# Re-timing a kernel of attention and two-layer products: first-block products among the first layer groups, scores behind quarters of w_out, batch 2's projection ten groups later with k and v loaded first

## The chip, the cores and the metric

One core of a Trainium2 chip. The metric is the device time of one execution in microseconds (us), median over runs. Executions are called fast when they are not in a slower state of the chip. "The trace" is one profiled execution; its span is some 1.8 us shorter than the time.

## The reference

```python
k_proj = einsum('ks,bhsd->bhkd', E, k)          # 1024 keys become 64
v_proj = einsum('ks,bhsd->bhkd', F, v)
attn   = softmax(q @ k_proj^T / 8) @ v_proj     # 8 batches, 8 heads, head size 64
x = attn, heads side by side                    # 8192 tokens x 512
h = x @ w_in                                    # 512 -> 2048
out = (h * clip(h + 3, 0, 6) / 6) @ w_out       # 2048 -> 512
```

All inputs are float32. The kernel computes in bfloat16 with float32 accumulation.

## The kernel before

Tokens go in blocks of 512, two to a batch. A **layer group** is four matmuls of one block against 128 columns of w_in, an activation on ScalarE (r) and a multiplication on VectorE (g); 16 groups make a block's first product. The second product (w_out) takes four rows of 16 matmuls, called here in **quarters** of four matmuls each. While batch b is multiplied, batch b+1's attention is spread between its groups by a generator: each `next(ahead)` is one **call**, one after each group and one after each row of w_out.

```python
ps_mm = ...tile_pool(name="ps_mm", bufs=4, PSUM)   # accumulators of the layer
ps_at = ...tile_pool(name="ps_at", bufs=4, PSUM)   # accumulators of the attention: pat()

class Attention:
    def project(self, ps): ...       # 8 matmul pairs: k and v to 64 rows, into one pat() tile
    def keys_out(self, ps): ...      # 2 VectorE copies of k out of that tile
    def values_out(self, ps): ...    # 2 VectorE copies of v out of that tile
    def scores(self, j, alloc): ...  # 8 matmuls into two pat() tiles, 2 exponentials on ScalarE
    def normalised(self, j):         # sums and values of one pair of heads: four pat() tiles
        den = self.quads(ones...); av = self.quads(vp...)
        lns = [log(den[t]) for t in range(NB)]
        yield
        for t in range(NB):
            nc.vector.tensor_mul(self.xT[:, j, t, :], av[t], inverse(lns[t]))
            yield
    def steps(self, plan):
        ps = pat(); self.project(ps)
        yield
        self.keys_out(ps); self.values_out(ps)
        yield
        self.keys_transposed_dma()                 # kT, a transposing DMA on SyncE's queue
        if self.b == 1: qT_dma[1] = q_transposed(1)
        if self.b + 1 < B:
            nc.gpsimd.tensor_copy(mark, ...)       # waits for qT (batch 1) or kT, then
            load_kqv(self.b + 1)                   # the next batch's q, k, v
        ...                                        # then the plan: (calls to wait, part, pair)

# first block of batch 0: fillers (matmuls on ones, thrown away) keep TensorE going
def busy(n): ...
    ...
    products(0); self.vals(1, nc.vector.tensor_copy); busy(2)
    products(1); self.vals(2, nc.scalar.copy); busy(2)
    products(2); self.vals(3, nc.scalar.copy); busy(2)
    products(3)
```

The softmax here doesn't subtract the row's maximum and nothing guards it: scores larger than these inputs give would overflow.

## Time and profile before

| | before |
|---|---|
| time, median of 4 | 525.78 us (525.38 to 526.23) |
| span of the trace | 523.8 us |
| TensorE busy | 510.6 us |
| idle TensorE apart from the first 1.5 us and the end (4.3), of which for v | some 7.4 us, 3.2 |
| mean granted clock | 0.997 |

A page line such as "PE 510.6 (97%) x2811" is busy time, share of the span and instructions. PE is TensorE, PEld its weight loads, DVE VectorE, ACT ScalarE, POOL GpSimd; L210 is line 210 of that run's kernel, so the same line has different numbers in different runs. A wait line gives engine, tile and line, what it waited for, the sum, the count and the longest. A timeline line gives start, duration, engine, source line, operation, output and inputs, shape and count, and in brackets the idle time before it with what ended it. The lines of the kernel before stand in the prediction.

### The profile page before, as it was taken

The page shows a single profiled execution, that of the slowest core. Times are in us where ns is not written, and L with a number is a line of the kernel's source. Part 1 is how long each engine was busy: PE and PEld are TensorE (multiplying, and loading weights), DVE is VectorE, ACT ScalarE, POOL GpSimd, SP SyncE. Part 2 cuts the span into 40 slices and gives each one's busy share as a digit, 9 for nine tenths or more (in the row PEclk, how much of TensorE's full clock was granted, in tenths as well). Part 3 has the DMA queues.
Part 4 walks back from the last instruction along what each step waited for, and adds up shares of the span by engine and source line. Part 5 has one row for each costly group of instructions (what it writes and reads, how often), then busy time and mean ns, then how long its engine had stood idle before and what let it go on. Part 6 is the DMA issues. An engine that isn't in the chain of part 4 may idle for free.

```text
span 523.8 us, 7239 instructions
## 1 busy us (share of the span) xinstructions
PE 510.6 (97%) x2811; PEld 223.9 (43%) x2811; DVE 237.9 (45%) x376; ACT 281.8 (54%) x518; POOL 37.3 (7%) x56
## 2 busy tenths in 40 slices
PE   8999989699999999999999999999999999999996
PEld 4444433344444444444444444444444444444442
DVE  3482734464553552553454454535435544444420
ACT  3565465296546763566436664467635765444431
POOL 8510020020020000200002000200000000000000
PEclk9999999899999999999999999999999999999999
DMA  9999699699229811595018941299111110111112
GB/s 173 202 205 207 137 161 216 127 150 161 73 58 199 176 43 40 93 218 122 32 38 144 186 97 40 56 190 182 46 41 31 41 41 21 41 41 42 40 41 80
DMA packets 73683, 55.40 MB, mean 106 GB/s; under 512 B 35504, under 2 KB 65456, under 8 KB 73648
## 3 DMA queue, kind: packets, MB, share of 16 engines
q0 software_dynamic: 31424, 29.36, 35.6%
q1 hardware_dynamic: 42000, 25.17, 18.6%
q8 instruction: 22, 0.36, 0.3%
q10 hardware_dynamic: 224, 0.39, 0.3%
q14 instruction: 13, 0.11, 0.1%
HBM read 59.24 MB, written 16.78 MB: 145 GB/s over the span
## 4 chain that ended last, share of the span: by engine, by line
PE 89%; DMA 5%; DVE 2%; ACT 1%; issue 1%; POOL 0%; SPq 0%; DVEq 0%; ACTq 0%
PE mm L402 40%; PE mm L422 39%; DMA v<-in_v_dram 4%; PE at L180 3%; PE at L216 2%; PE mm L84 1%; PE at L202 1%; DMA qT<-q 1%; DVE g L408 1%; PE at L320 0%; DVE kp L186 0%; ACT r L407 0%; ACT ln L158 0%; PE at L272 0%; PE at L288 0%
## 5 line engine op out<-in xcount | busy, mean ns | idle before, releaser
L408 DVE SCALAR_TENSOR_TENSOR g<-r,mm 128x512 bf16<-128x512 f32 x256 | 172.4, 685 | 215.7 <-ACT r L407 215.3
L402 PE MATMUL mm<-xT,w_in_sb 128*128 128x512 bf16 x1024 | 236.4, 380 | 1.3 <-DVE g L408 1.3
L422 PE MATMUL mm<-w_out_sb,g 128*128 128x512 bf16 x1024 | 231.3, 379 | 0.0
L407 ACT ACTIVATE r<-mm 128x512 f32<-128x512 f32 x256 | 152.0, 604 | 70.8 <-PE mm L402 68.2
L402 PEld LDWEIGHTS <-w_in_sb 128*128 128x128 bf16 x1024 | 97.1, 98 | 126.7 <-issue 15.6
L422 PEld LDWEIGHTS <-g 128*128 128x128 bf16 x1024 | 98.9, 98 | 121.1 <-issue 3.8
L436 ACT COPY o_sb<-mm 128x512 f32<-128x512 f32 x59 | 34.5, 585 | 143.4 <-PE mm L422 143.4
L227 DVE TENSOR_TENSOR xT<-at,rec 128x512 bf16<-128x512 f32 x56 | 38.0, 684 | 24.3 <-ACT rec L163 24.3
L163 ACT ACTIVATE rec<-ln 128x512 f32<-128x512 f32 x60 | 37.6, 638 | 0.0
L158 ACT ACTIVATE ln<-at 128x512 f32<-128x512 f32 x60 | 33.0, 615 | 7.6 <-PE at L216 4.5
L207 ACT ACTIVATE aT<-at 128x512 bf16<-128x512 f32 x56 | 28.9, 611 | 2.3 <-PE at L202 2.3
L244 POOL COPY mark<-kT 1x1 bf16<-1x1 bf16 x5 | 0.9, 176 | 250.0 <-DMA kT<-kp 250.0
L180 PE MATMUL at<-v,f_t 128*64 128x512 bf16 x56 | 14.6, 407 | 3.2 <-DMA v<-in_v_dram 3.2
L180 PE MATMUL at<-k,e_t 128*64 128x512 bf16 x56 | 14.6, 404 | 0.0
L216 PE MATMUL at<-aT,vp 64*64 64x512 bf16 x112 | 12.3, 378 | 0.4 <-DVE xT L227 0.2
L84 PE MATMUL mm<-ones 128*128 128x512 bf16 x27 | 10.1, 482 | 1.5 <-DVE ones L77 1.5
L216 PE MATMUL at<-aT,ones 64*64 64x512 bf16 x112 | 11.5, 400 | 0.0
L180 PEld LDWEIGHTS <-e_t 128*64 128x64 bf16 x56 | 5.8, 113 | 10.2 <-issue 6.5
L202 PE MATMUL at<-qT,kT 64*64 64x256 bf16 x224 | 8.8, 275 | 1.3 <-DMA qT<-q 1.3
L190 DVE CAST vp<-at 64x512 bf16<-64x512 f32 x14 | 9.7, 694 | 0.3
L186 DVE CAST kp<-at 64x512 bf16<-64x512 f32 x14 | 8.9, 674 | 0.0
L216 PEld LDWEIGHTS <-ones 64*64 64x64 bf16 x112 | 3.2, 103 | 11.9 <-issue 11.9
(57 smaller groups left out, 110.2 us busy)
## 6 DMA issues: line engine op xcount, KB each, us to landing
out_dram<-o_sb SPq DMA_DIRECT2D x63, 256.0 KB, 2.0
k<-in_k_dram POOLq DMA_DIRECT2D x7, 1024.0 KB, 15.0
v<-in_v_dram POOLq DMA_DIRECT2D x7, 1024.0 KB, 20.5
q<-in_q_dram POOLq DMA_DIRECT2D x7, 1024.0 KB, 9.9
w_out_sb<-in_moe_w_out_dram POOLq DMA_DIRECT2D x4, 512.0 KB, 17.7
w_in_sb<-in_moe_w_in_dram POOLq DMA_DIRECT2D x3, 512.0 KB, 12.1
k<-in_k_dram POOLq DMA_DIRECT2D x4, 256.0 KB, 5.4
v<-in_v_dram POOLq DMA_DIRECT2D x4, 256.0 KB, 7.5
```

The source lines that it names most:

```text
L84: nc.tensor.matmul(ps, ones[:, :P], ones, start=True, stop=True)
L158: nc.scalar.activation(ln, den, AF.Ln)
L163: nc.scalar.activation(rec, ln, AF.Exp, scale=-1.0)
L180: nc.tensor.matmul(ps[e * KP:(e + 1) * KP], ef_t[e][:, so, :], kqv[self.b]["kv"[e]][:, :, so, :], start=(so == 0), stop=(so == SO - 1))
L207: nc.scalar.activation(self.aT[j][:, r].rearrange("p a n -> p (a n)"), tiles[r], AF.Exp, scale=scale)
L216: nc.tensor.matmul(tiles[t][c:c + D].rearrange("p (r n) -> p r n", r=2), stationary(r, 2 * j + a), self.aT[j][r:r + KP, :, a, :], start=Tr ...
L227: nc.vector.tensor_mul(self.xT[:, j, t, :], av[t], inverse(lns[t]))
L402: nc.tensor.matmul(h_ps, w_in_sb[:, ko, fo * P:(fo + 1) * P], xT[:, ko, t, :], start=(ko == 0), stop=(ko == KO - 1))
L407: nc.scalar.activation(r, h_ps, AF.Relu, bias=0.5, scale=1.0 / 6.0)
L408: nc.vector.scalar_tensor_tensor(g[:, fo, :], r, 1.0, h_ps, op0=ALU.min, op1=ALU.mult)
L422: nc.tensor.matmul(o_ps, g[:, fo, c * P:(c + 1) * P], w_out_sb[:, fo, :], start=(fo == 0), stop=(fo == FO - 1))
L436: (copy or nc.scalar.copy)(o_sb, o_ps)
```

## The change

Four things are intended: real work instead of fillers in the first block, scores asked for later so that VectorE and the transposing DMA have finished, batch 2's v landed before it is projected, and VectorE's copies out of the projection spread out. The plan becomes a table of parts with the number of calls to wait before each.

```diff
+            if self.b + 1 < B:
+                mark = ...
+                load_kqv(self.b + 1, "qkv" if self.b > 1 else "kvq")
...
+    PLANS = {1: ((0, "project"), (0, "keys_out"), (1, "turn"), (0, "values_out", 0), (2, "values_out", 1),
+                 (1, "two_scores", 0), (3, "two_scores", 2), (1, "normalised", 0),
+                 (0, "normalised", 1), (0, "normalised", 2), (0, "normalised", 3)),
+             2: ((10, "project"), (0, "keys_out"), (1, "turn"), (2, "values_out", 0), (3, "values_out", 1),
+                 (1, "two_scores", 0), (2, "two_scores", 2), (3, "normalised", 0),
+                 (0, "normalised", 1), (1, "normalised", 2), (0, "normalised", 3))}
...
             scores(KO - 1)
+            self.vals(0, nc.vector.tensor_copy)
             sums(KO - 2)
-            busy(1)
-            self.vals(0, nc.vector.tensor_copy)
+            self.vals(1, nc.vector.tensor_copy)
+            products(0)
             sums(KO - 1)
...
+            products(2)
             self.vals(3, nc.scalar.copy)
-            busy(2)
+            yield                       # the last product comes between the first groups' matmuls
             products(3)
...
-    first.second_scores()
+    ahead = Attention(1, x_next).steps(PLANS[1])
     rows = [second_group(0, 0, g[0], c) for c in range(SB)]
     for i in range(SB + 1):
         for c in range(SB - 1):
             next(rows[c], None)
-        if i < 2:
-            first.second_values(2 * i)
+        if i == 0:
+            first.second_scores()
+        elif i < 3:
+            first.second_values(2 * i - 2)
...
-        if c == 1:
-            qT_dma[2] = q_transposed(2)
+    qT_dma[2] = q_transposed(2)         # after the four rows
```

Batches 3 to 7 keep their plan.

More of the change, by code (lines that the diff above doesn't have):

```diff
@@ L173, in __init__, with project @@
             self.vp = att.tile([P, H, D], bf16, tag="vp", name="vp")
-            self.qT, self.aT = {}, {}
-        def project(self, ps):
+            self.aT = {}
+        def project(self):
+            ps = self.ps = pat()
             for so in range(SO):
@@ L182, in project, with keys_out, values_out, turn @@
                                      start=(so == 0), stop=(so == SO - 1))
-        def keys_out(self, ps):
+        def keys_out(self):
             for a in range(2):
-                nc.vector.tensor_copy(self.kp[:, :, a, :], ps[:KP].rearrange("p (h d) -> p h d", d=D))
-        def values_out(self, ps):
-            for a in range(2):
-                nc.vector.tensor_copy(self.vp[a * KP:(a + 1) * KP], ps[KP:].rearrange("p (h d) -> p h d", d=D))
-        def keys_transposed_dma(self):
-            nc.sync.dma_start_transpose(self.kT, self.kp.rearrange("p h a d -> p (h a d)"))
-        def scores(self, j, alloc):
+                nc.vector.tensor_copy(self.kp[:, :, a, :], self.ps[:KP].rearrange("p (h d) -> p h d", d=D))
+        def values_out(self, a):
+            nc.vector.tensor_copy(self.vp[a * KP:(a + 1) * KP], self.ps[KP:].rearrange("p (h d) -> p h d", d=D))
+        def turn(self):
+            nc.sync.dma_start_transpose(self.kT, self.kp.rearrange("p h a d -> p (h a d)"))
+            if self.b == 1:
+                qT_dma[1] = q_transposed(1)
+            if self.b + 1 < B:
+                mark = att.tile([1, 1], bf16, tag="mark", name="mark")
+                nc.gpsimd.tensor_copy(mark, self.kT[:1, 0, :1] if self.b > 1 else qT_dma[1][:1, 0, 0, :1])
+                load_kqv(self.b + 1, "qkv" if self.b > 1 else "kvq")
+        def scores(self, j):
+            qT = qT_dma[self.b]
             self.aT[j] = att.tile([P, 2, 2, HT], bf16, tag="aT", name="aT", bufs=KO + 1)
-            tiles = [alloc() for _ in range(2)]
+            tiles = [pat() for _ in range(2)]
             for a in range(2):
@@ L203, in scores @@
                                          self.kT[r * D:(r + 1) * D, 2 * j + a, :],
-                                         self.qT[j][r * D:(r + 1) * D, a, t * HT:(t + 1) * HT],
+                                         qT[r * D:(r + 1) * D, j, a, t * HT:(t + 1) * HT],
                                          start=True, stop=True)
@@ L228, in normalised, with two_scores @@
                 yield
+        def two_scores(self, j):
+            self.scores(j)
+            self.scores(j + 1)
         def steps(self, plan):
-            ps = pat()
-            self.project(ps)
-            yield
-            self.keys_out(ps)
-            self.values_out(ps)
-            yield
-            self.keys_transposed_dma()
-            if self.b == 1:
-                qT_dma[1] = q_transposed(1)
-            if self.b + 1 < B:
-                mark = att.tile([1, 1], bf16, tag="mark", name="mark")
-                nc.gpsimd.tensor_copy(mark, self.kT[:1, 0, :1] if self.b > 1 else qT_dma[1][:1, 0, 0, :1])
-                load_kqv(self.b + 1)
-            self.qT = {j: qT_dma[self.b][:, j] for j in range(KO)}
-            for wait, what, j in plan:
+            for wait, part, *args in plan:
                 for _ in range(wait):
                     yield
-                if what == "scores":
-                    self.scores(j, pat)
-                    self.scores(j + 1, pat)
-                else:
-                    yield from self.normalised(j)
-    LATER = ((6, "scores", 0), (3, "values", 0), (1, "values", 1),
-             (1, "scores", 2), (3, "values", 2), (1, "values", 3))
+                yield from getattr(self, part)(*args) or ()
+    PLAN = ((0, "project"), (1, "keys_out"), (0, "values_out", 0), (0, "values_out", 1), (1, "turn"),
+            (6, "two_scores", 0), (3, "normalised", 0), (1, "normalised", 1),
+            (1, "two_scores", 2), (3, "normalised", 2), (1, "normalised", 3))
+    PLANS = {1: ((0, "project"), (0, "keys_out"), (1, "turn"), (0, "values_out", 0), (2, "values_out", 1),
[4 more added lines that the diff above has]
+                 (0, "normalised", 1), (1, "normalised", 2), (0, "normalised", 3))}
     class First:
@@ L360, in first_block @@
                 self.keys_transposed(j)
-                busy(1)
+                if j < 2:
+                    busy(1)
             scores(KO - 1)
+            self.vals(0, nc.vector.tensor_copy)
             sums(KO - 2)
-            busy(1)
-            self.vals(0, nc.vector.tensor_copy)
-            sums(KO - 1)
-            busy(1)
-            products(0)
-            self.vals(1, nc.vector.tensor_copy)
-            busy(2)
-            products(1)
-            self.vals(2, nc.scalar.copy)
-            busy(2)
+            self.vals(1, nc.vector.tensor_copy)
+            products(0)
+            sums(KO - 1)
+            self.vals(2, nc.vector.tensor_copy)
+            products(1)
+            busy(1)
             products(2)
             self.vals(3, nc.scalar.copy)
-            busy(2)
+            yield
             products(3)
@@ L451, with two_groups @@
     first = First(xT)
-    first.first_block()
+    by_pairs = first.first_block()
+    next(by_pairs)
     x_next = x_tile()
-    ahead = Attention(1, x_next).steps(((1, "scores", 0), (3, "scores", 2), (1, "values", 0),
-                                        (0, "values", 1), (0, "values", 2), (0, "values", 3)))
     g = [g_tile(), g_tile()]
-    early = [pmm(), pmm()]
-    for kos in (range(KO - 1), range(KO - 1, KO)):
+    def two_groups(t, kos, more):
+        tiles = [pmm(), pmm()]
+        for i, (fo, part) in enumerate([(fo, part) for part in kos for fo in range(2)]):
+            h_part(tiles[fo], xT, t, fo, part)
+            if i == 0:
+                more()
         for fo in range(2):
-            h_part(early[fo], xT, 0, fo, kos)
-    for fo in range(2):
-        h_out(early[fo], g[0], fo)
+            h_out(tiles[fo], g[t], fo)
+    two_groups(0, ((0, 1), (2,), (3,)), lambda: next(by_pairs, None))
     for fo in range(2, FO):
         first_group(xT, 0, g[0], fo)
-        if fo in (13, 14):
-            first.queries(1, (0, 1) if fo == 13 else (2, 3))
-    first.second_scores()
+        if fo >= FO - 2:
+            first.queries(1, (0, 1) if fo == FO - 2 else (2, 3))
+    ahead = Attention(1, x_next).steps(PLANS[1])
     rows = [second_group(0, 0, g[0], c) for c in range(SB)]
@@ L471 @@
             next(rows[c], None)
-        if i < 2:
-            first.second_values(2 * i)
-    for fo in range(FO):
+        if i == 0:
+            first.second_scores()
+        elif i < 3:
+            first.second_values(2 * i - 2)
+    two_groups(1, ((0, 1), (2, 3)), lambda: None)
+    for fo in range(2, FO):
         first_group(xT, 1, g[1], fo)
-        if fo == 7:
-            next(ahead)
-        elif fo == 8:
-            next(ahead)
+        if fo in (7, 8, 9, 10):
             next(ahead)
@@ L482 @@
             whole(rows[3])
-    next(ahead)
     for c in range(SB):
@@ L497 @@
             x_next = x_tile()
-            ahead = Attention(b + 1, x_next).steps(LATER if b > 1 else (
-                (6, "scores", 0), (5, "scores", 2), (4, "values", 0),
-                (1, "values", 1), (1, "values", 2), (1, "values", 3)))
+            ahead = Attention(b + 1, x_next).steps(PLANS.get(b + 1, PLAN))
         for t in range(NB):
```

## The prediction

> **What bounds the kernel now.** I read the page first: its totals, its slices and the chain that ended last.
>
> ```profile
> PE 510.6 (97%) x2811; PEld 223.9 (43%) x2811; DVE 237.9 (45%) x376; ACT 281.8 (54%) x518; POOL 37.3 (7%) x56
> PE 89%; DMA 5%; DVE 2%; ACT 1%; issue 1%; POOL 0%; SPq 0%; DVEq 0%; ACTq 0%
> ```
>
> TensorE is busy for 510.6 of 523.8 us and makes 89% of the chain, so only three things can shorten the kernel: gaps on TensorE, matmuls that do no needed work, and time at a lower clock. The gaps sum to 523.8 - 510.6 = 13.2 us. The table of stretches puts none after 140 us except in the end (19.7 busy of the last 24.0 us, so 4.3); the diff leaves the end alone. So the change plays out in the first 140 us. Next, the waits of TensorE:
>
> ```profile
> PE at L180 <- DMA v<-in_v_dram: 3.2, 1, 3.2
> ...
> PE at L202 <- DMA qT<-q: 1.3, 1, 1.3
> PE mm L402 <- DVE g L408: 1.3, 1, 1.3
> ```
>
> The largest is batch 2's projection waiting for v. The timeline of TensorE shows what follows it (start, duration, instruction, in brackets the idle time before):
>
> ```profile
> 90.71 0.40 PE L180 MATMUL at<-k,e_t 128*64 128x512 bf16 x1
> 94.33 0.38 PE L180 MATMUL at<-v,f_t 128*64 128x512 bf16 x1 [3.22 <-DMA v<-in_v_dram]
> ...
> 96.80 0.63 PE L180 MATMUL at<-v,f_t 128*64 128x512 bf16 x1
> 97.37 4.91 PE L402 MATMUL mm<-xT,w_in_sb 128*128 128x512 bf16 x20
> 103.57 2.75 PE L402 MATMUL mm<-xT,w_in_sb 128*128 128x512 bf16 x12 [1.30 <-DVE g L408]
> ```
>
> The wait for v is paid three times: the gap, matmuls of 0.63 instead of 0.38 us after it, and a second gap of 1.30 us. The table of stretches of 1 us gives the clock (last but two of the columns):
>
> ```profile
> 95.00:96.00 1.00, 1.00 (x7) 0.53 (x5) 0.00 (x0) 0.00 (x0) 0.00 (x0) 0.50 1.28 290
> 96.00:97.00 1.00, 1.00 (x7) 0.36 (x3) 0.00 (x0) 0.00 (x0) 0.00 (x0) 0.50 1.19 338
> ```
>
> VectorE's timeline explains the second gap: four copies out of the projection (1.27 and 1.40 us) stand in front of the next g:
>
> ```profile
> 100.09 1.27 DVE L186 CAST kp<-at 64x512 bf16<-64x512 f32 x2
> 101.40 1.40 DVE L190 CAST vp<-at 64x512 bf16<-64x512 f32 x2
> 102.83 3.12 DVE L408 SCALAR_TENSOR_TENSOR g<-r,mm 128x512 bf16<-128x512 f32 x5
> ```
>
> **What the Trainium skill says.** "TensorE: Matmul & The Clock Gate", Part 1 (the HAM clock gate): after an idle window of about 3.4 us the array runs at half its clock until a busy window of such length has passed, and matmuls of 512 columns then start every 426.7 ns instead of 215.7. This trace agrees: 94.33 - 90.92 = 3.41 us without a start, then a clock of 0.50 for about 3 us and pairs of matmuls about 0.43 apart instead of 0.215. "DMA: Bandwidth & Descriptors", section "Issuing engines are not separate DMA queues": transfers of all issuers interleave on the same 16 engines. The trace agrees: batch 1's qT, with no load beside it, lands 6.8 us after issue; batch 2's, beside the loads of k and v, 13.9. "Perfetto Trace Analysis", "Optimization Strategy", advises to find the gaps of the limiting engine and what they wait on; that is the order used above.
>
> **The change part by part.** A layer group of the first product is four matmuls: 56 of them start between 22.30 and 34.40, so 0.216 each and 0.863 a group.
>
> *Front.* From the third pair on, 10 filler matmuls on ones go and one is put back: 9 x 0.216 = 1.9 us. The last pair's products move between the first two groups' partial sums, so their wait is covered. How much arrives is set by the weights. From the DMA view of narrow windows, issue time plus time to landing:
>
> ```profile
> w_in_sb<-in_moe_w_in_dram POOLq DMA_DIRECT2D x1, 128.0 KB, 9.2
> w_in_sb<-in_moe_w_in_dram POOLq DMA_DIRECT2D x1, 512.0 KB, 10.8
> ```
>
> The first piece lands at 10.65 + 9.2 = 19.85, the first of 512 KB (groups 4 to 7) at 13.40 + 10.8 = 24.2. Walking the new order with the old durations, and with the old waits for ScalarE's exponentials at 13.8 and 16.1, I get the first pair's values at 15.5, the third's product at 18.65 to 18.95, its last v product done at 19.5; then the first group waits for w_in to 19.95. Partial sums, last product, two whole groups follow: 20 matmuls or so, group 4 is wanted at 23.8 and must wait to about 24.3. Before, it began at 22.30 + 4 x 0.863 = 25.75. **Gain 1.45 us**; the rest of the removed fillers turns into waits for w_in. The queue is full from 3 us on (about 205 GB/s) and its order is unchanged, so no weight lands earlier. Later pieces (26.7, 29.25; w_out from 34.4) come in time.
>
> *Block 1's scores of batch 0* waited 0.36 us for VectorE's copy of q, and the scores cost 1.11 us from 37.11 to 38.22 for 16 matmuls that take 0.57 without the wait. Behind a quarter of w_out (12 matmuls, 2.6 us) the copy is done. **Gain 0.5.** Sum 2.0, so block 1 begins near 47.9, batch 1's projection near 54.8 (its v is in at 26.96 + 25.2 = 52.2).
>
> *Batch 1's scores* came 1.32 us too early for qT:
>
> ```profile
> 70.62 0.63 PE L202 MATMUL at<-qT,kT 64*64 64x256 bf16 x16 [1.32 <-DMA qT<-q]
> ```
>
> Copying k right behind the projection puts the transposition of k near 58 to 59 us. Batch 1's q lands at 29.53 + 30.3 = 59.8, so qT is issued at 59.9 and lands at 66.7 instead of 70.5. TensorE reaches the scores, now one quarter (0.86) later in order, at 56.6 + 8 x 0.863 + 3.45 + 0.86 = 67.8. **Gain 1.3**, 1.1 us to spare.
>
> *Batch 2's projection.* Its loads start on qT's arrival, 67 instead of 71, k and v first. Before, the first load took 9.6 us and the second landed 5.7 us after it, so v is in at about 83. Batch 1's layer then begins near 89.75 - 3.3 = 86.4, the projection ten groups in: 86.4 + 11 x 0.863 = 95.9, 13 us to spare. What goes: from 90.71 to 97.37 are 6.66 us for a projection that takes 1.85 undisturbed (145.30 to 147.15), 4.8 lost; then the 20 matmuls from 97.37 to 103.57 take 6.2 us where 20 later ones (from 106.82) took 4.42, 1.8 lost. **Gain 6.6.** The k copies now run while the next group fills (0.86 + ScalarE's 0.60 cover their 1.27), the v copies (0.69 each) come three groups apart; with four accumulator buffers TensorE waits only when g is late by over 3 x 0.863 - 0.60 - 0.69 = 1.3 us. I do not expect that.
>
> Sum 1.45 + 0.5 + 1.3 + 6.6 = 9.85, and 0.1 to 0.4 for small gaps lost or won. All later layers keep their plan. 525.8 - 9.9 = **515.9 us**, or 0.981 of before: just short of 2%.
>
> **Rivals.** (1) *The front gives all of its fillers*, 1.9 instead of 1.45, if w_in is no limit: 515.4. Against it: the landing times and a full queue. (2) *The late plan makes a new wait*: batch 2's scores need kT, which queues on SyncE behind qT. q now comes last and lands near 89; issue takes 4.9 us alone, 11.8 beside loads. kT is wanted on the queue at about 99 and the scores at 103.6, so alone it fits; if q's landing slipped by 8 us, TensorE would stand 1 to 3 us: 517 to 519. Likewise four exponentials (2.06 us) before the next r delay it by about 1.2 us, at the edge of the buffers: at most 0.3 us. (3) *A cold clock in front*: without fillers a gap of over 3 us would halve the clock for 3.4 us and cost 1.7: 517.6. Against it: the gaps I find there are of 0.6 us at most, and 1.32 us before the scores did not lower the clock. (4) *The wait for v was hidden anyway*: no; no engine or queue holds TensorE between 104 and 140, so what is saved is not given back. (5) *The bound passes to VectorE or ScalarE* in batch 1's second half, where scores and values of batch 2 are crowded: ScalarE has about 25 us of work there (16 r, 4 outputs, 24 exps and logs at 0.5 to 0.6) for some 31 us of TensorE, so a few tenths at worst.
>
> **Range and chances.** Low end: all of it and the full fillers, with 0.4 of small waits won, 515.0. High end: a new wait of 1.5 us in the crowded plan, 517.6. The threshold of 2% is 515.3, 0.6 below my value, and what could bring more than 9.85 is small: faster 0.16. A loss by over 2% would need 20 us of new stalls: 0.01. The rest, 0.83, within 2%.
>
> **What would show it.** Right: no wait of TensorE for v; clock 1.0 from 10 to 140 us; group 4 of the first block held by w_in to about 24.3; batch 1's scores near 68 without a wait for qT; batch 2's projection near 96 with matmuls of 0.38 us; no wait for g after it; busy TensorE near 507 us; the stretch after 140 us unchanged, some 10 us earlier. Wrong: a new wait at the scores of batch 2 (kT or qT), at g in the crowded half, or a half clock in the front.

## The result

The changed kernel takes **518.36 us** (517.99 to 518.49, 4 runs) against 525.78. The ratio of the two is 0.9858 (95% interval 0.984 to 0.9875); a ratio here is the mean time of one kernel's fast runs over that of the other's of the same rounds, so not quite the ratio of the medians. The gain is 7.4 us where 9.9 were predicted, and the time lies outside the predicted range, 0.76 us over its high end.

The totals and TensorE's waits of the changed kernel, from its page and its table of waits:

```profile
PE 502.4 (97%) x2752; PEld 222.7 (43%) x2802; DVE 239.4 (46%) x377; ACT 282.0 (55%) x517; POOL 37.2 (7%) x56
```

```profile
PE mm L401 <- DMA w_in_sb<-in_moe_w_in_dram: 1.0, 2, 0.7
PE at L210 <- DVE vp L190: 0.9, 1, 0.9
PE at L224 <- ACT ln L158: 0.8, 1, 0.8
```

The waits for batch 2's v, for qT and for g are gone. Three new lines stand in their place, besides two of 0.3 us in the front. (This trace lacks records of some matmuls, 1001 of 1024 in the first product, so busy TensorE is a little low; starts of groups are the safer measure.) The timeline of TensorE shows where the new waits lie:

```profile
20.37 0.38 PE L401 MATMUL mm<-xT,w_in_sb 128*128 128x512 bf16 x1 [0.66 <-DMA w_in_sb<-in_moe_w_in_dram]
...
24.60 9.67 PE L401 MATMUL mm<-xT,w_in_sb 128*128 128x512 bf16 x43 [0.35 <-DMA w_in_sb<-in_moe_w_in_dram]
...
68.40 0.63 PE L210 MATMUL at<-qT,kT 64*64 64x256 bf16 x16
...
104.25 0.51 PE L210 MATMUL at<-qT,kT 64*64 64x256 bf16 x9
105.64 0.41 PE L210 MATMUL at<-qT,kT 64*64 64x256 bf16 x7 [0.88 <-DVE vp L190]
105.98 1.90 PE L401 MATMUL mm<-xT,w_in_sb 128*128 128x512 bf16 x8
...
123.62 0.41 PE L224 MATMUL at<-aT,ones 64*64 64x512 bf16 x4
123.86 0.85 PE L224 MATMUL at<-aT,vp 64*64 64x512 bf16 x4
124.64 3.63 PE L421 MATMUL mm<-w_out_sb,g 128*128 128x512 bf16 x16
...
129.92 0.41 PE L224 MATMUL at<-aT,ones 64*64 64x512 bf16 x4
131.44 0.40 PE L224 MATMUL at<-aT,vp 64*64 64x512 bf16 x2 [0.85 <-ACT ln L158]
131.78 1.90 PE L401 MATMUL mm<-xT,w_in_sb 128*128 128x512 bf16 x8
```

The first two lines are the front, held by w_in as predicted. Batch 1's scores at 68.40 wait for nothing. The rest belongs to batch 2's attention: seven of the score matmuls wait 0.88 us, four value matmuls take 0.85 us instead of 0.39 (a wait hidden inside a merged line), two wait 0.85. The timelines of VectorE and ScalarE in the changed kernel have the instructions that can end the longer waits:

```profile
104.89 0.69 DVE L190 CAST vp<-at 64x512 bf16<-64x512 f32 x1
...
130.65 0.68 DVE L235 TENSOR_TENSOR xT<-at,rec 128x512 bf16<-128x512 f32 x1
...
130.78 1.09 ACT L158 ACTIVATE ln<-at 128x512 f32<-128x512 f32 x2
```

104.89 + 0.69 = 105.58, and TensorE goes on at 105.64, 0.06 us later. For the second wait two come into question. The multiplication on VectorE ends at 130.65 + 0.68 = 131.33; the first of the two logarithms takes 0.61 us and ends at 131.39. TensorE goes on at 131.44. The wait table, which goes by semaphores, names the logarithm, and the 0.05 us from its end fit the 0.06 above. So the accumulator that these matmuls waited for was one that the same pair's sums had just filled.

A ledger of starts in the two traces tells which step of the sum failed:

| start of | before | after | gained so far | gained in the step | predicted for it |
|---|---|---|---|---|---|
| group 4 of the first block | 25.75 (22.30 + 4 x 0.863) | 24.60 | 1.15 | 1.15 | 1.45 |
| block 1's first product | 49.92 | 48.22 | 1.70 | 0.55 | 0.5 |
| batch 1's layer | 89.75 | 86.66 | 3.09 | 1.39 | 1.3 |
| batch 2's layer | 144.27 | 136.97 | 7.30 | 4.21 | 6.6 |
| end of the span | 523.8 | 516.5 | 7.3 | 0.0 | 0 |

2.4 of the missing 2.5 us are in one row: batch 1's layer, in which batch 2's attention is prepared. It took 54.52 us before and 50.31 after; 47.9 was predicted.

One thing about the kernel before bears on the size of the gain. Of its 23 executions timed beside the experiments, 18 took 525.0 to 526.4 us with a granted clock of 0.992 to 0.997, as in the trace, and 5 took 523.5 to 524.3 with a clock of 1.000. So the half clock was not in every execution. What decided it isn't known, since no trace of the five was kept.

### The profile page after: what moved, and what is told of

Read it like the earlier page. It is cut to its first block, busy times and chain, and to the rows that moved or that the text cites. A ratio compares the mean times of both kernels' runs of the same rounds, so it can differ in the third digit from the quotient of the medians.

```text
span 516.5 us, 7173 instructions
## 1 busy us (share of the span) xinstructions
PE 502.4 (97%) x2752; PEld 222.7 (43%) x2802; DVE 239.4 (46%) x377; ACT 282.0 (55%) x517; POOL 37.2 (7%) x56
## 4 chain that ended last, share of the span: by engine, by line
PE 89%; DMA 3%; ACT 2%; issue 2%; DVE 2%; POOL 1%; another core or an unknown queue 0%; DVEq 0%; ACTq 0%; POOLq 0%
PE mm L421 41%; PE mm L401 41%; PE at L224 3%; PE at L181 3%; DMA w_in_sb<-in_moe_w_in_dram 2%; PE at L210 1%; DMA k<-in_k_dram 1%; DVE g L407 1%; ACT ln L158 0%; ACT r L406 0%; POOL q L97 0%; ACT aT L215 0%; POOL k L101 0%; DVE xT L235 0%
## 5 line engine op out<-in xcount | busy, mean ns | idle before, releaser
L401 PE MATMUL mm<-xT,w_in_sb 128*128 128x512 bf16 x1001 | 232.5, 379 | 3.4 <-issue 1.7
L181 PE MATMUL at<-k,e_t 128*64 128x512 bf16 x56 | 13.4, 382 | 0.0
L181 PE MATMUL at<-v,f_t 128*64 128x512 bf16 x56 | 13.4, 382 | 0.0
L84 PE MATMUL mm<-ones 128*128 128x512 bf16 x18 | 7.0, 521 | 1.5 <-DVE ones L77 1.5
```

Of the source, the lines that this page charges most:

```text
L181: nc.tensor.matmul(ps[e * KP:(e + 1) * KP], ef_t[e][:, so, :], kqv[self.b]["kv"[e]][:, :, so, :], start=(so == 0), stop=(so == SO - 1))
L401: nc.tensor.matmul(h_ps, w_in_sb[:, ko, fo * P:(fo + 1) * P], xT[:, ko, t, :], start=(ko == 0), stop=(ko == KO - 1))
```

## The experiments

**Theories.** A: the three late waits are for one of the four attention accumulators (`pat()`), each still being read by VectorE when the next part asks for it. B: ScalarE or VectorE is overloaded in this half however the parts are arranged. C: the ten groups of delay are what took away the wait for v. D: the earlier start of the loads alone did. Each run was timed in five rounds against the kernel before, whose medians in the three calls were 525.29, 525.14 and 525.37 us. Because runs on different chips differ by tenths, the table also has the length of batch 1's layer in the trace, which the front cannot change.

| run | time (us) | ratio to before | batch 1's layer (us) |
|---|---|---|---|
| changed kernel, again | 518.18 | 0.9868 | 50.31 |
| v_copy_sooner | 517.65 | 0.9862 | 49.71 |
| v_copy_later | 518.0 | 0.9868 | 50.16 |
| last_pair_later | 517.18 | 0.9853 | 49.38 |
| project_at_once | 517.24 | 0.9852 | 49.24 |
| q_first | 518.36 | 0.9871 | 50.31 |
| q_first_at_once | 519.23 | 0.9883 | 51.77 |
| old_front | 519.74 | 0.9898 | 50.31 |
| front_w | 518.19 | 0.9869 | 50.31 |
| spread | 515.5 | 0.9819 | 47.47 |
| best | 514.37 | 0.9797 | 47.48 |

All were correct. The edits below are against the changed kernel; those of the plan are in batch 2's.

### v_copy_sooner

```diff
-(3, "values_out", 1), (1, "two_scores", 0)
+(2, "values_out", 1), (2, "two_scores", 0)
```

> Changed kernel with batch 2's second v copy one call earlier (after the last group of the half before), its scores where they were. Theory A (the four attention accumulators go round: the fourth tile of the scores is the projection's, held until that copy): the wait of 0.88 us at batch 2's scores falls below 0.2, 517.5 us. Rival B (ScalarE's four exponentials in a row hold up the groups, the accumulators don't matter): wait and time unchanged, 518.4.

Measured 517.65 us; the layer got 0.60 shorter. TensorE's timeline of this run:

```profile
104.23 0.51 PE L210 MATMUL at<-qT,kT 64*64 64x256 bf16 x9
105.03 0.41 PE L210 MATMUL at<-qT,kT 64*64 64x256 bf16 x7 [0.28 <-DVE vp L190]
```

The wait fell from 0.88 to 0.28, exactly the amount by which the layer shortened, with the exponentials where they were. That speaks for A and against B. It did not fall below 0.2 as expected: the copy now ended only at 104.97.

### v_copy_later

```diff
-(3, "values_out", 1), (1, "two_scores", 0)
+(4, "values_out", 1), (0, "two_scores", 0)
```

> The same copy one call later, right before the scores. Theory A: the wait at batch 2's scores grows by one group, 0.86 us, to 1.7, and the time to 519.2. Rival B: unchanged, 518.4.

A miss: 518.0 us, and the wait did not grow. By its number this run fits B, which expected no change. TensorE's timeline of this run:

```profile
104.08 0.51 PE L210 MATMUL at<-qT,kT 64*64 64x256 bf16 x9
105.32 0.41 PE L210 MATMUL at<-qT,kT 64*64 64x256 bf16 x7 [0.73 <-ACT aT L215]
```

TensorE stops at the same place, after nine matmuls, but is released by an exponential instead of the v copy, which in this run ended only at 106.22. So the tile it waited for cannot have been the projection's; it must be one that the first scores had just filled. From this I infer that which of the four accumulators comes next is not fixed by the order in the program, as theory A had assumed. The fourth pair's wait for a logarithm in the changed kernel points the same way. How they are handed out was not tested further and stays open. It is a wait for an accumulator either way, since all that the exponential shares with these matmuls is the accumulator it reads; but this run does not show its size as a function of the distance.

### last_pair_later

```diff
-(0, "normalised", 3)
+(1, "normalised", 3)
```

> Changed kernel with the last pair's sums and values of batch 2 one group later. Theory A (its second values tile waits for the multiplication that reads the pair before): the wait of 0.85 us falls below 0.2, 517.5 us. Rival B (ScalarE is overloaded in this half, logarithms come late wherever they stand): wait moves but stays at 0.5 or more, 518.2 or more; if the multiplication is then too late for the next layer's first group, a wait for xT of up to 1 us.

Measured 517.18 us, the layer 0.93 shorter. TensorE's timeline of this run:

```profile
130.83 0.41 PE L224 MATMUL at<-aT,ones 64*64 64x512 bf16 x4
131.07 0.77 PE L224 MATMUL at<-aT,vp 64*64 64x512 bf16 x4
```

The wait of 0.85 us is gone from the table of waits; 0.77 instead of 0.39 us for the four value matmuls is what remains, as with the third pair. That 0.38 lies between the two expectations (below 0.2 for A, 0.5 or more for B), and the time is nearer to A's. ScalarE does the same work in the same half, so this too speaks against B. The instruction awaited is now another one:

```profile
130.70 0.68 DVE L235 TENSOR_TENSOR xT<-at,rec 128x512 bf16<-128x512 f32 x1
...
131.43 0.10 PEld L224 LDWEIGHTS <-vp 64*64 64x64 bf16 x1 [0.47 <-issue]
```

The last weight load of the pair comes at 131.43, when VectorE's multiplication has just ended (131.38). So what A expected the pair to wait for holds here, but in the changed kernel it was the logarithm.

### project_at_once

```diff
-(10, "project"), ... (1, "two_scores", 0)
+(0, "project"), ... (11, "two_scores", 0)
```

> Changed kernel with batch 2's projection and copies ten groups earlier, scores and later parts at the same calls. Theory A: v landed at 83.6 us, the projection comes at 87.5, so no wait for v; the v copies are done long before the scores, so the 0.88 us goes and 0.85 and 0.45 stay: 517.5 us. Rival C (the ten groups are what took away the wait for v): a wait of TensorE for v of 1 us or more, 519.5 or more.

Measured 517.24 us, the layer 1.07 shorter, and no wait for v at the projection in its table of waits (the 0.5 us for v that it lists belong to the front). The scores ran without a break in it:

```profile
104.31 0.63 PE L210 MATMUL at<-qT,kT 64*64 64x256 bf16 x16
```

So the ten groups of delay were not needed beside the new load order, and cost about 1 us, because they brought the v copies next to the scores. C falls for the changed kernel as it stands.

### q_first and q_first_at_once

```diff
-load_kqv(self.b + 1, "qkv" if self.b > 1 else "kvq")
+load_kqv(self.b + 1, "qkv")
```

The first has only this edit, the second also the plan of project_at_once.

> Changed kernel with batch 2 loaded q, k, v again, projection still ten groups late. If the lateness alone removes the wait for v (theory A): v lands near 89.4 us, the projection comes at 96.2, no wait, time as the changed kernel, 518.3. Rival C (the order of the loads is needed): a wait for v of over 0.5 us, 519 or more.

> Batch 2 loaded q, k, v and projected at its first group: both means undone, the loads still starting at 67 us. Theory A: v lands near 89.4, the projection stands at 87.6, a wait of about 1.8 us, too short for the half clock: about 2 us over the run project_at_once (517.2), so 519.2. Rival D (the earlier start of the loads alone suffices): no wait, 517.2.

Measured 518.36 and 519.23 us. q_first has the same layer as the changed kernel, 50.31 us. The table of waits of q_first_at_once:

```profile
PE at L181 <- DMA v<-in_v_dram: 2.2, 1, 2.2
```

Its layer is 2.53 us longer than project_at_once's. So either means alone, the load order or the delay, removes the wait for v, and with neither it returns: D falls. It is 2.2 us and not 3.2 because the loads start some 4 us earlier than before and the projection comes 3 us earlier. The table of stretches of q_first_at_once also shows that after this gap, unlike after the one of 3.2 us in the trace before, the clock stays at 1.00 (the last column but two):

```profile
91.00:92.00 1.00, 1.00 (x11) 0.47 (x7) 0.00 (x0) 0.00 (x0) 0.00 (x0) 1.00 1.27 279
92.00:93.00 1.00, 1.00 (x6) 0.42 (x6) 0.78 (x2) 0.00 (x0) 0.00 (x0) 1.00 1.24 219
```

### old_front

The first block's tail with its fillers as before, everything else changed.

> Changed kernel with the first block's products and fillers as before. Theory A (new front worth what w_in's arrival leaves, 1.15 us by the two traces): group 4 of the first block starts near 25.9 instead of 24.6, time 519.6. Rival (the fillers' full 1.9 us): 520.3. Rival (front hidden behind later transfers): 518.4.

Measured 519.74 us, 1.4 more than the changed kernel, with batch 1's layer unchanged. Group 4 starts at 22.49 + 16 x 0.216 = 25.95 in its trace, 1.35 later than in the changed kernel's. The front is worth what w_in's arrival leaves, not the 1.9 us of the fillers, and nothing later hides it.

### front_w

```diff
-    for j in range(KO): load_pair("v", j)
+    for j in range(KO - 1): load_pair("v", j)
...
+    load_w_in(0, 128)
+    load_pair("v", KO - 1)
-    for lo, n in ((0, 128), (128, 128), (256, 256), (512, 512), ...):
+    for lo, n in ((128, 128), (256, 256), (512, 256), (768, 256), ...):
```

> Changed kernel with the first piece of w_in loaded before the last pair's v, and the first piece of 512 KB cut in two. If w_in's arrival bounds the new front: the waits of 0.66 and 0.35 us for w_in go, group 4 starts near 23.9 instead of 24.6, 517.7 us. Rival (the front is bound by its chain of ScalarE and VectorE): group 4 unchanged, 518.3.

Half a miss: 518.19 us. TensorE's timeline of this run:

```profile
19.87 0.62 PE L291 MATMUL at<-v,f_t 128*128 128x128 bf16 x8 [0.81 <-DMA v<-in_v_dram]
...
21.19 12.74 PE L403 MATMUL mm<-xT,w_in_sb 128*128 128x512 bf16 x58
```

Cutting the piece of 512 KB in two removed the second wait (58 matmuls run on from 21.19; group 4 starts near 21.19 + 14 x 0.216 = 24.2, 0.4 sooner). Swapping the first piece of w_in with the last pair's v bought nothing: the first wait, 0.81 us, is now for v. Nor does its name mean much, since with the order unswapped it falls on w_in in some traces (0.66 in the changed kernel's) and on v in others (0.6 in v_copy_sooner and q_first). That what bounds the front is the sum of bytes before both, in one full queue, whatever their order, fits this but is argued, not shown. The total moved by only 0.2 us, within the spread of the runs; the trace shows batch 1's layer at 86.32, 0.34 us earlier than in the changed kernel's, where runs with an unchanged front have 86.49 to 86.88.

### spread, best and the changed kernel again

```diff
-2: ((10, "project"), (0, "keys_out"), (1, "turn"), (2, "values_out", 0), (3, "values_out", 1),
-    (1, "two_scores", 0), (2, "two_scores", 2), (3, "normalised", 0),
-    (0, "normalised", 1), (1, "normalised", 2), (0, "normalised", 3))
+2: ((3, "project"), (0, "keys_out"), (1, "turn"), (1, "values_out", 0), (2, "values_out", 1),
+    (4, "two_scores", 0), (2, "two_scores", 2), (3, "normalised", 0),
+    (1, "normalised", 1), (2, "normalised", 2), (2, "normalised", 3))
```

best has this, the cut of w_in from front_w without the swap, and in batch 1's plan

```diff
-(3, "two_scores", 2), (1, "normalised", 0)
+(2, "two_scores", 2), (2, "normalised", 0)
```

> Changed kernel with batch 2's plan spread: projection four groups in (v landed at 83.6, wanted at 90.1), v copies at the 6th and 8th call, scores at the 12th and 14th, each pair's values right after a stretch of the second product (17th, 21st, 26th, 31st). Theory A (2.2 us of waits for attention accumulators are what the prediction missed): waits of 0.88, 0.85 and the hidden 0.45 go, no new one for kT (lands near 97, wanted at 98.9), 516.2 us. Rival B (ScalarE or VectorE is overloaded in batch 1's layer however it is arranged): 517.2 or more, with a wait for g or r.

> The spread plan, with the first 512 KB of w_in cut in two (the wait of 0.35 us before group 4 goes) and batch 1's scores and values each two quarters apart (0.5 us of waits for accumulators after the second scores go): 515.4 us, 2.9 under the changed kernel. If the two quarters are not the cause of that stretch, 515.9.

> The changed kernel again, on the same chip as the two above: 518.3 us, all theories.

Measured 515.5, 514.37 and 518.18 us. In spread, the table of waits has none for TensorE in batch 1's layer; TensorE's timeline of spread where the waits were:

```profile
98.94 0.63 PE L210 MATMUL at<-qT,kT 64*64 64x256 bf16 x16
99.51 1.90 PE L399 MATMUL mm<-xT,w_in_sb 128*128 128x512 bf16 x8
...
118.97 0.41 PE L224 MATMUL at<-aT,ones 64*64 64x512 bf16 x4
119.21 0.39 PE L224 MATMUL at<-aT,vp 64*64 64x512 bf16 x4
119.53 3.63 PE L399 MATMUL mm<-xT,w_in_sb 128*128 128x512 bf16 x16
...
126.78 0.39 PE L224 MATMUL at<-aT,vp 64*64 64x512 bf16 x4
```

All value matmuls take 0.39 us, and the layer takes 47.47 us, 2.84 less than the changed kernel's. The bracketed idle times (0.88 and 0.85, and the hidden 0.46) sum to only 2.19. Starts give the whole, since they also count what is lost in the matmuls around a gap. From the first scores to the next group are 1.73 us in the changed kernel and 0.57 here (98.94 to 99.51). From the sums of the third and fourth pair to what follows are 1.02 and 1.86 there and 0.56 here (118.97 to 119.53). The three cost 1.16 + 0.46 + 1.30 = 2.92 us; the second scores take 0.09 more here (101.34 to 102.00, instead of 0.57), which leaves 2.83. B falls: the same work on all engines fits without these waits.

best takes off another 1.1 us: in its trace block 1's first product starts 0.38 us earlier than in spread (47.71 against 48.09, the cut of w_in; runs with the uncut piece have 48.05 to 48.44) and the stretch from there to batch 1's layer is 0.83 shorter (37.62 against 38.45, the two quarters; 0.5 was expected). best is 11 us under the kernel before, ratio 0.9797 (0.9776 to 0.9817, so the verdict at 2% is "unclear", as it is for spread), and 3.8 under the changed kernel of the same call. It still has one such wait in batch 1's attention, last pair: 82.44 to 83.60 by starts, 1.16 us instead of 0.56.

## Why the prediction was wrong

- **Front**: right in mechanism. Group 4 was held by w_in, at 24.60 where 24.3 was predicted: the whole trace is some 0.2 us later from the start (the first key projection at 7.78 instead of 7.57), and 24.2 for the piece's arrival became 13.4 + 11.1 = 24.5. old_front confirms the value.
- **Block 1's scores and batch 1's scores**: right, 0.55 and 1.39 us for 0.5 and 1.3.
- **Batch 2's projection: the step that failed.** The three losses did go (no wait for v, no half clock, no wait for g), as predicted, so 6.6 us were there to be won. But of the late plan the prediction said of waits that it did "not expect that", and of the crowded half, "at most 0.3 us". It counted only the layer's four accumulators and the load of ScalarE. It left out the other four, the attention's. After a group's matmuls end, VectorE reaches a copy placed behind that group only after r and g: in the changed kernel the v copy ended about 2.3 us after the matmuls of the group before it (103.3 to 105.58), and the multiplication that the third pair waits for at 124.25, about 2.5 us after those of its group (121.79). The plan asks for the accumulator one group (0.86 us) or two groups later. The rest of that time TensorE stands. The fourth pair finds all four accumulators taken as well, and there the one it got was that of its own sums, after the logarithm on ScalarE (131.39; the multiplication of the pair before it ended at 131.33). By the starts the three cost 1.16, 0.46 and 1.30 us, 2.92 together. The value predicted allowed for none of this, the rivals for a few tenths, and only the high end of the range for 1.5. The kernel before already lost 0.46 in this way, hidden in the line of its last pair, which took 133.90 - 132.88 = 1.02 us instead of 0.56:

```profile
132.88 0.41 PE L216 MATMUL at<-aT,ones 64*64 64x512 bf16 x4
133.12 0.84 PE L216 MATMUL at<-aT,vp 64*64 64x512 bf16 x4
133.90 3.63 PE L422 MATMUL mm<-w_out_sb,g 128*128 128x512 bf16 x16
```

So the new plan added 2.46 us, and 6.6 - 4.21 = 2.39 are missing in the ledger's row: the two agree within 0.1. v_copy_sooner and last_pair_later each shortened one of these waits, and spread removed all three. A fifth accumulator for the attention, the direct test of the shortage, was not tried.
- **Rival 2** named the right place (the crowded plan, 517 to 519) but the wrong wait: kT and qT were in time (qT issued at 89.42 and landed 6.6 us later, 8 us before the scores; kT landed at 102.3, 2 us before them).
- **The delay itself** was taken as needed; project_at_once shows that the load order was enough, with v in at 68.03 + 15.6 = 83.6 us against a projection at 87.5. The prediction had both numbers (v "at about 83", the layer at 86.4) and did not draw the conclusion.
- **A reading that was off**: the "3.41 us without a start" of the prediction. The last matmul before the gap starts at 90.71, so 3.62 us pass without a start, and the idle time in brackets is 3.22. The trace has no start at 90.92. So the agreement claimed there is rougher than 3.41 suggests; no step of the sum rests on it.

With spread the time comes to 515.5, next to the predicted 515.9. That is partly luck: spread also removed the 0.46 us that the kernel before had lost unnoticed, and the front gave 0.3 less than predicted.

## What to carry to other kernels

When parts of one computation are threaded between the groups of another, count for each buffer how long after the matmuls of the group before it its last reader ends (here 2.3 us: two engines in turn, then the reader itself) and put the next request at least that far behind, best after a stretch that gives those engines nothing to do. Check every pool, not only that of the main loop. A wait can hide inside a merged line of the timeline: compare starts, not only the idle times listed. And when two cures are put on one wait, try each alone: the second may cost something and buy nothing.

## What the Trainium skill lacked or had wrong

- "Perfetto Trace Analysis", "Optimization Strategy", takes a gap that repeats for a stretch as a possible sign of too few buffers. Here the shortage of accumulators showed as three single gaps (0.88, 0.46, 0.85 us), and moving the requests removed them without another buffer (spread).
- "DMA: Bandwidth & Descriptors", "Measured (HBM→SBUF, 128 partitions, SWDGE, issued from GpSimd)", does not say which side's bytes count in a load that converts. Here pieces of 512 KB in bfloat16 landed every 2.5 us (24.2, 26.7 and 29.25 us): about 205 GB/s written, so about 410 GB/s read as float32, near that table's 425 only if the source is counted.
- The same page, "Latency and other measured facts", gives 261 GB/s for a transposing DMA with a strided middle dimension and 350 to 400 otherwise. Here qT, 1 MB, took 6.6 us from issue to landing with no load beside it, some 159 GB/s with its fixed part, and 13.9 us beside loads.
